# Attention outputs of a delta-rule kernel computed already transposed, in two column tiles, with their last rows moved by DMA

## The chip, the core and the metric

The kernel runs on one core of one Trainium2 chip. A core has TensorE (PE: matmuls; PEld: its weight loads), VectorE (DVE), ScalarE (ACT), GpSimd (POOL) and SyncE (SP), which only issues DMAs here. Each engine works through its own queue in order, and semaphores tie the queues together. TensorE writes to PSUM only; ScalarE and VectorE copy from PSUM to SBUF. The metric is the device time of one launch in microseconds.

## The reference

Two blocks run one after the other. The first is a delta rule over 4 batches x 8 heads, 768 steps, with heads 48 wide; the second is an MLP on its outputs.

```python
k_n = k / (norm(k) + 1e-6)
for t in range(768):
    y[t] = q[t] @ state                       # 48 x 48 state of each head
    v_old = state.T @ k_n[t]
    state += beta[t] * outer(k_n[t], v[t] - v_old)
x = y with heads side by side                 # 3072 tokens x 384
h = x @ w_in                                  # 384 x 2048
out = (h * sigmoid(1.702 * h)) @ w_out        # 2048 x 384
```

w_in and w_out arrive as 64-bit floats (numpy makes them so), and the kernel converts them to fp32 on the chip. q, k, v and beta are fp32.

## The kernel before, in words

**Units.** The sequence is cut into 6 chunks of 128 steps. A *unit* is one chunk of one batch with its 8 heads, so there are 24 units, in the order chunk by chunk, four batches in each. Within a chunk the recurrence is a triangular system. It is solved in four blocks of 32 rows with the inverses of the 32x32 diagonal blocks.

**Per unit.** `prepare` transposes K and Q of the unit (L285) and computes their products G (psG, L299). It sends G out to DRAM and back as NT (L311, L317), so that the blocks of two units lie one per partition. `invert` inverts them on VectorE, in 15 steps for halves of 16x16 (L363, L367) and then products of the halves (L346, L347); the last step YS (L397) goes to DRAM and comes back as XB (L401, L406). One call inverts two units; with the first chunk it is all four.

The class `Step` then walks through a unit. `keys` (L427) puts K times the state into psR. For each block `above` (L438) adds the blocks above to psR, `rest` (L446, VectorE) subtracts psR from V, and `solve` (L450) multiplies V by the inverse; `solved` (L457, ScalarE) copies the result to U. `queries` puts Q times the state into psY, `state` (L469, L477) updates S_bd, and `outputs` (L481) adds G times U to psY. psY has 128 tokens as rows and 8 heads x 48 as columns. ScalarE copies it to x (L486). `transposed` then transposes x in three pieces of 128 columns (L491), and VectorE copies them to xT (L493). xT holds 384 features in three pieces of 128 partitions, for the 256 tokens of a pair of units.

The state S_bd of two heads is block diagonal, 128 x 96, so that one matmul of `with_state` serves two heads. The heads of a pair lie at partitions 0 to 47 and 64 to 111; the partitions between are zero.

**The MLP.** `hidden` (ph, L506) multiplies w_in by xT, with w_in as weights and 256 tokens as data (128 for the first pair), and ScalarE applies the activation (L511). `written` (po, L521) multiplies by w_out. VectorE copies the result (L528), and a DMA writes it out (L529).

**Order.** The outer loop runs over *slots*, 26 of them. Slot n works on three units at once: the last two blocks and the outputs of unit n-1 (A), the second block of unit n (B_), and the start of unit n+1 (D_). It also prepares unit n+4. In even slots from 2 to 20 it also spreads an inversion over its groups. A slot has seven *groups*. After the attention work of a group the loop takes MLP work from a queue: `take(todo / (7 - group))` with `share` = 20.8 us of it in a slot, by costs written in the code (1.3 per two matmuls of po or three of ph). Outputs are group 5, transposes group 6. After every second slot `hidden` of the finished pair and then `written` are appended to the queue.

The order in the source is not yet the order on the engines: a scheduling layer reorders instructions of all engines by its own estimates, except those wrapped in `pinned`. The order is fixed when the program is built.

**Weights.** w_in comes in 12 parts of 128 rows x 512 columns and w_out in 16 parts of 128 x 384, fetched by DMA (L215) into space that is still free. Each is converted by five operations on VectorE and one on ScalarE (`from_double`, L164 to L173). This goes on during the first slots. Dummy matmuls `warm` (L135) keep TensorE's clock up where there is no other work.

Of the kernel before, what the change touches and what calls it, by code (L numbers as in the profile page):

```python
# [18 lines left out]
def kernel(  # L19
# [19 lines left out]
    nc = tc.nc  # L39
# [10 lines left out]
    BS = 32  # L50
    NB = C // BS
    HB = 2
    NTH = HB * C
    FQ = 4
    GB = 4
# [2 lines left out]
    NA = W0  # L58

    NW, NA0, NY, NB0 = 80, 3, 48, 6  # L60
    NS = C * C + C
    assert S % C == 0 and H == 8 and D <= DP and DM == H * D == KC * 128
    assert B == 4 and B * H * NB == 128 and FC == 4 * FQ

    cpool = ctx.enter_context(tc.tile_pool(name="const", bufs=1))
    io = ctx.enter_context(tc.tile_pool(name="io", bufs=3))
# [109 lines left out]
    parts_in = KC * DFF // N_IN  # L176
    n_parts = parts_in + FC

    stages, taken = {}, {}

    def stage(part):
# [15 lines left out]
    def fetch(part, dma):  # L197

        if part < parts_in:
            j, f0 = part % KC, part // KC * N_IN  # L200
            src = moe_w_in[j * 128 : (j + 1) * 128, f0 : f0 + N_IN]
        else:
            f = part - parts_in
            src = moe_w_out[f * 128 : (f + 1) * 128, :]
        if src.dtype == F32:
            dma(out=target(part), in_=src)
        else:
            if (s := stage(part)) is None:
                raw = wk.tile([128, DM, 2], I32, tag="xT", name="raw", bufs=3)
            else:  # L210
                taken[part] = s
                raw = w_out.rearrange("p f d -> p (f d)")[:, s[0] : s[1]].bitcast(I32)
                raw = raw.rearrange("p (n o) -> p n o", o=2)
            stages[part] = raw
            dma(  # L215
                out=raw.bitcast(src.dtype).rearrange("p n o -> p (n o)"), in_=src
            )

    def target(part):
        if part < parts_in:  # L220
# [193 lines left out]
    class Step:  # L414
# [40 lines left out]
        def solved(self, blk, psU):  # L455
            r = slice(blk * BS, (blk + 1) * BS)
            nc.scalar.copy(self.U[r], psU[r])  # L457

        def queries(self):
            self.psY = bank("psY")  # L460
            if self.c > 0:
                self.with_state(self.psY, 1)

        def state(self):
            if self.c == NC - 1:
# [11 lines left out]
                nc.vector.tensor_tensor(St, psS[pr, :, hh, :], St, op=ALU.add)  # L477

        def outputs(self):
            for h in range(H):  # L480
                nc.tensor.matmul(  # L481
                    self.psY[:, h, :], lhsT=self.G[:, h, 1, :], rhs=self.U[:, h, :],
                    start=(self.c == 0 and h == 0), stop=True, skip_group_check=True,
                )
            self.x = wk.tile([128, DM], F32, tag="o", name="x")
            nc.scalar.activation(self.x, self.psY.rearrange("p h d -> p (h d)"), ACT.Copy)  # L486

        def transposed(self):
            psX = bank("psXT2", (128, KC, 128))
            for j in range(KC):  # L490
                nc.tensor.transpose(psX[:, j, :], self.x[:, j * 128 : (j + 1) * 128], ident)  # L491
            i = self.b % HB
            nc.vector.tensor_copy(self.xT[:, :, i * C : (i + 1) * C], psX)  # L493


    def hidden(xT, gT, t, cost):
# [73 lines left out]
    def slot(n, share):  # L570

        nonlocal inverting
        A, B_, D_ = steps.pop(n - 1, None), steps.get(n), None
        P = prepare(n + B) if B <= n + B < len(units) else iter(())
        m = n - HB
        if m >= 0 and m % HB == 0 and m + B < len(units):  # L580
            inverting = invert(*units[m + B], HB)
        left = WB[n + 1] if n + 1 < len(WB) else 0
        todo = share
        for group in range(7):
            if group == 0:
                if A:
                    for h in range(H):
                        A.above(2, h)
                    A.rest(2)
                next(P, None)  # L590
            elif group == 1:
                psU = bank("psU") if A else None
                for h in range(H):
                    if A:
                        A.solve(2, h, psU)
                    if B_:
                        B_.above(1, h)
                if A:
                    A.solved(2, psU)
                if B_:  # L600
                    B_.rest(1)
                next(P, None)
            elif group == 2:
                if A:
                    for h in range(H):
                        A.above(3, h)
                    A.rest(3)
                if n + 1 < len(units):
                    h = (n + 1) // HB
                    if h not in xTs:  # L610
                        xTs[h] = wk.tile([128, KC, NTH], F32, tag="xT", name="xT", bufs=3)
                    D_ = steps[n + 1] = Step(n + 1, xTs[h])
                    D_.keys()
                    D_.rest(0)
            elif group == 3:
                psU = bank("psU")
                turns = [(X, blk) for X, blk in ((A, 3), (B_, 1), (D_, 0)) if X]
                for h in range(H):
                    for X, blk in turns:
                        X.solve(blk, h, psU)  # L620
                for X, blk in turns:
                    X.solved(blk, psU)
                if A:
                    A.queries()
                next(P, None)
            elif group == 4:
                if A:
                    A.state()
                next(P, None)
                run(P)  # L630
            elif group == 5:
                if A:
                    A.outputs()
            elif A:
                A.transposed()
            ahead_of(inverting, 4)
            more = left // (7 - group)
            run(weights(more))
            left -= more
            if queue:  # L640
                for cost in take(todo / (7 - group)):
                    todo -= cost
            if not queue and n <= HB:
                warm(NB0)
        if n + 1 == len(WB) - 1:
            run(weights(n_parts))
        run(inverting)
        if n > 0:
            if n - 1 + B < len(units):
                load_values(n - 1 + B)  # L650
            m = n - 1 + len(KN)
            if m < len(units):
                load(m, ((KN, k), (QP, q)), sync if n < B else nc.sync.dma_start)
                normalize(m, nc.gpsimd.tensor_tensor)
            h = (n - 1) // HB
            if h == 0:
                i = (n - 1) % HB
                queue.append(hidden(xTs[h], gT0, slice(i * C, (i + 1) * C), 0.67))
            if n % HB == 0:
                gT = gT0 if h == 0 else []  # L660
                if h > 0:
                    queue.append(hidden(xTs[h], gT, slice(0, NTH), 1.3))
                queue.append(written(*units[h * HB], gT))
                xTs.pop(h)
# [29 lines left out]
        normalize(i, nc.gpsimd.tensor_tensor)  # L694
    run(weights(W1))
    for n in range(-1, len(units) + 1):
        slot(n, 20.8)
    run(take(1e9))


# [28 lines left out]
```

## Time and profile before

Median of 3 runs: 877.55 us (876.33 to 877.77). The profiled run took 876.47, its span is 874.6.

| what | from the page or an answer of the trace |
|---|---|
| busy share of PE, PEld, DVE, ACT, POOL | 95%, 72%, 56%, 23%, 12% |
| po L521, ph L506 | 267.5 us and 264.6 us of PE |
| outputs psY L481 | 384 records, 45.3 us; their weight loads 46.5 us |
| queries psY L427 | 160 records, 22.6 us |
| transposes psXT L491 | 72 records, 11.9 us |
| x copy L486 (ACT), xT copy L493 (DVE) | 24 x 489 ns, 24 x 552 ns |
| HBM to SBUF of a w_in part | 12 DMAs of 512 KB, 5.3 us to land |
| granted clock over the span | 0.973 (lower only at the start) |

How to read it. A matmul in fp32 appears as two records, so 24 units x 8 heads give 384 records in L481. The ends of PE records are modelled, so the distance from one start to the next tells more than the busy time. The number after a line's name counts records. A wait written in brackets at the end of a line names the engine and line that ended it.

### The profile page before, as it was taken

The numbers are of one execution on the slowest core, as the hardware profiler recorded it, in microseconds if no ns is written. First come the engines' busy times: TensorE is split into PE (matmuls) and PEld (weight loads), VectorE is DVE, ScalarE is ACT, GpSimd is POOL, SyncE is SP. The second block draws the span as 40 slices with busy tenths as digits, with TensorE's granted clock in tenths as the row PEclk, the third lists the DMA queues.
The fourth block names the chain that finished last, engine by engine and source line by source line (L and its number), as shares of the span: only waits on it lengthen the run. The fifth ranks groups of instructions, "written<-read, shape, count | busy, mean of one in ns | idle before, by whom it ended". The sixth has DMA issues, their size and how long they took to land.

```text
span 874.6 us, 15165 instructions
## 1 busy us (share of the span) xinstructions
PE 829.1 (95%) x6506; PEld 631.2 (72%) x6506; DVE 491.6 (56%) x1020; ACT 198.7 (23%) x363; POOL 102.2 (12%) x92
## 2 busy tenths in 40 slices
PE   8228999999999999999999999999999999999998
PEld 7116787668768768768768768768768778677684
DVE  7898889878871592591592591592591580110100
ACT  3103433332213213213213213113113112112020
POOL 2101111220030120120120120120100000000000
PEclk9659999999999999999999999999999999999999
DMA  9835643541222222222222232221121110000000
GB/s 239 211 60 116 163 134 85 128 103 31 53 70 40 49 58 52 49 66 44 49 61 49 48 70 41 48 64 40 38 61 31 31 40 13 10 10 1 10 10 18
DMA packets 159299, 54.56 MB, mean 62 GB/s; under 512 B 127232, under 2 KB 154880, under 8 KB 159232
## 3 DMA queue, kind: packets, MB, share of 16 engines
q1 hardware_dynamic: 153104, 52.38, 25.8%
q10 hardware_dynamic: 6128, 1.21, 1.0%
q8 instruction: 51, 0.84, 0.4%
q14 instruction: 16, 0.13, 0.1%
HBM read 33.13 MB, written 20.45 MB: 61 GB/s over the span
## 4 chain that ended last, share of the span: by engine, by line
PE 87%; DVE 11%; issue 1%; DMA 1%; POOL 0%; ACT 0%; SPq 0%; DVEq 0%; POOLq 0%
PE po L521 29%; PE ph L506 27%; PE psG L299 5%; PE psR L438 5%; PE psY L481 4%; PE psU L450 4%; PE psT L285 3%; PE psR L427 2%; PE psY L427 2%; PE ps_warm L135 2%; PE psS L469 2%; DVE P L101 1%; DVE YB L101 1%; PE psXT L491 1%; DVE tmp L172 1%; DVE P L346 1%
## 5 line engine op out<-in xcount | busy, mean ns | idle before, releaser
L521 PE MATMUL po<-w_out,gT 128*128 128x384 f32 x768 | 267.5, 494 | 0.0
L506 PE MATMUL ph<-xT,w_in 128*128 128x256 f32 (+1 forms) x1248 | 264.6, 366 | 0.2 <-DVE xT L493 0.2
L506 PEld LDWEIGHTS ph<-xT,w_in 128*128 128x128 f32 x1248 | 217.8, 191 | 30.4 <-issue 5.3
L521 PEld LDWEIGHTS po<-w_out,gT 128*128 128x128 f32 x768 | 139.7, 190 | 86.4 <-issue 6.1
L446 DVE TENSOR_TENSOR V<-V,psR 32x384 f32<-32x384 f32 x92 | 50.7, 551 | 135.8 <-PE psR L438 130.3
L511 ACT ACTIVATE gT<-ph 128x512 f32<-128x512 f32 (+1 forms) x104 | 58.6, 564 | 218.6 <-PE ph L506 218.5
L135 PE MATMUL ps_warm<-ident 128*128 128x256 bf16 x290 | 42.3, 306 | 36.3 <-DVE ps_warm L101 33.2
L323 POOL TENSOR_SCALAR_AFFINE_SELECT G<-G 128x1024 f32<-128x1024 f32 x24 | 27.0, 1126 | 385.2 <-DVE G L307 150.9
L457 ACT COPY U<-psU 32x384 f32<-32x384 f32 x96 | 45.1, 469 | 113.7 <-PE psU L450 61.6
L438 PEld LDWEIGHTS psR<-U,G 32*32 32x32 f32 (+2 forms) x1152 | 53.1, 108 | 19.0 <-issue 18.5
L135 PEld LDWEIGHTS <-ident 128*128 128x128 bf16 x290 | 31.0, 110 | 45.1 <-DVE ps_warm L101 34.3
L438 PE MATMUL psR<-U,G 32*32 32x48 f32 (+2 forms) x1152 | 62.7, 206 | 0.0
L299 PE MATMUL psG<-kqT 48*128 48x256 f32 x384 | 59.6, 402 | 2.9 <-ACT G L303 1.9
L450 PEld LDWEIGHTS psU<-V,XB 32*32 32x32 f32 x1536 | 37.5, 106 | 24.9 <-issue 9.1
L493 DVE COPY xT<-psXT 128x384 f32<-128x384 f32 x24 | 13.3, 552 | 70.6 <-PE psXT L491 70.4
L307 DVE COPY G<-psG 128x512 f32<-128x512 f32 x44 | 30.2, 689 | 40.3 <-PE psG L299 39.8
L363 DVE TENSOR_TENSOR P<-NT,YB 64x2 f32<-64x2 f32 (+4 forms) x150 | 49.1, 327 | 4.7
L367 DVE TENSOR_REDUCE YB<-P 64x2 f32<-64x2 f32 (+4 forms) x150 | 48.0, 320 | 4.7
L481 PEld LDWEIGHTS psY<-U,G 128*128 128x128 f32 x384 | 46.5, 192 | 4.4 <-ACT U L457 0.8
L450 PE MATMUL psU<-V,XB 32*32 32x48 f32 x1536 | 44.7, 204 | 2.3 <-DVE V L446 2.2
L299 PEld LDWEIGHTS psG<-kqT 48*128 48x128 f32 x384 | 36.2, 186 | 14.4 <-ACT G L303 3.1
L286 ACT ACTIVATE kqT<-psT 128x512 f32<-128x512 f32 x48 | 28.2, 600 | 76.7 <-PE psT L285 74.1
(78 smaller groups left out, 712.2 us busy)
## 6 DMA issues: line engine op xcount, KB each, us to landing
Nd<-G SPq DMA_DIRECT2D x24, 512.0 KB, 3.2
w_out<-in_moe_w_in_dram SPq DMA_DIRECT2D x12, 512.0 KB, 5.3
w_out<-in_moe_w_out_dram SPq DMA_DIRECT2D x14, 384.0 KB, 3.3
KN<-in_k_dram SPq DMA_DIRECT2D x24, 192.0 KB, 2.8
V<-in_v_dram SPq DMA_DIRECT2D x24, 192.0 KB, 3.2
out_dram<-o SPq DMA_DIRECT2D x24, 192.0 KB, 2.0
QP<-in_q_dram SPq DMA_DIRECT2D x21, 192.0 KB, 3.0
NT<-Nd SPq DMA_DIRECT2D x24, 128.0 KB, 2.5
```

What stands on the lines that cost most here:

```text
L135: nc.tensor.matmul(ps, lhsT=ones[:, 0:128], rhs=ones, start=True, stop=True)
L299: nc.tensor.matmul(ps[hh][:, i], lhsT=kqT[pr, g + i, 0, :], rhs=kqT[pr, g + i, :, :], start=True, stop=True,)
L363: tt(P, diag(Nf, i * BS, [[0, i], [1, i]]), diag(Yf, 0, [[BS, i], [1, i]]), op=ALU.mult,)
L367: red(diag(Yf, i, [[BS, i]]), P, axis=AX.X, op=ALU.add, negate=True)
L438: nc.tensor.matmul(self.psR[r, h, :], lhsT=self.G[a, h, 0, r], rhs=self.U[a, h, :], start=(self.c == 0 and h == 0), stop=True, skip_group_ ...
L446: nc.vector.tensor_tensor(self.V[r], self.V[r], self.psR[r], op=ALU.subtract)
L450: nc.tensor.matmul(psU[r, h, :], lhsT=self.XB[r, h, :], rhs=self.V[r, h, :], start=True, stop=True,)
L457: nc.scalar.copy(self.U[r], psU[r])
L481: nc.tensor.matmul(self.psY[:, h, :], lhsT=self.G[:, h, 1, :], rhs=self.U[:, h, :], start=(self.c == 0 and h == 0), stop=True, skip_group_ ...
L506: nc.tensor.matmul(ph[:, u], lhsT=w_in[:, j, f * 128 : (f + 1) * 128], rhs=xT[:, j, t], start=(j == 0), stop=(j == KC - 1),)
L511: nc.scalar.activation(gT[f0 // FQ][:, f0 % FQ : f0 % FQ + 2, t], ph, ACT.Gelu_apprx_sigmoid)
L521: nc.tensor.matmul(po, lhsT=gT[f // FQ][:, f % FQ, i * C : (i + 1) * C], rhs=w_out[:, f, :], start=(f == 0), stop=(f == FC - 1),)
```

## The change

psY is made transposed at once: 48 features of a head as rows and 128 tokens as columns. For this U, and in the queries the state, become the weights, and G or Q the data. Even heads write partitions 0 to 47, odd heads partitions 64 to 111, by turns: two column tiles of TensorE. So x, the transposes and their PSUM bank go, and a slot has six groups instead of seven.

psY has four pieces of 96 used rows, but xT has three of 128. The first three pieces go to xT by one copy per half (ScalarE the even heads, VectorE the odd ones). Heads 6 and 7, the fourth piece, are first copied to a tile `last` and then moved by six DMAs of 16 rows x 128 tokens to the free partitions 48 to 63 and 112 to 127 of the three pieces. The rows of w_in have to lie in the same order, so each of its parts comes in four DMAs (48, 16, 48 and 16 rows). In the first slots `share` is smaller, 15.6 and then 18.8, so that MLP work is kept for later slots.

```diff
+    GR = 6
+    XR = DP - D
+    def x_rows(j):
+        return [
+            (p + o, r, m)
+            for hh in range(2)
+            for p in (hh * 64,)
+            for o, r, m in (
+                (0, (2 * j + hh) * D, D),
+                (D, (2 * KC + hh) * D + j * XR, XR),
+            )
+        ]
...
-            dma(
-                out=raw.bitcast(src.dtype).rearrange("p n o -> p (n o)"), in_=src
-            )
+            raw = raw.bitcast(src.dtype).rearrange("p n o -> p (n o)")
+            for p, r, m in rows:
+                dma(out=raw[p : p + m], in_=src[r : r + m])
...
+        def turned(self, lhsT, rhs, start):
+            for h in range(H):
+                j, p = h // 2, h % 2 * 64
+                nc.tensor.matmul(
+                    self.psY[p : p + D, j, :], lhsT=lhsT(h), rhs=rhs(h),
+                    start=start and j == 0, stop=True, skip_group_check=True,
+                )
+
         def queries(self):
-            self.psY = bank("psY")
+            self.psY = bank("psY", (128, NP, 128))
             if self.c > 0:
-                self.with_state(self.psY, 1)
+                self.turned(
+                    lambda h: S_bd[h % 2 * 64 : h % 2 * 64 + D, self.b, h // 2, h % 2, :],
+                    lambda h: self.kqT[h % 2 * 64 : h % 2 * 64 + D, h // 2, 1, :],
+                    True,
+                )
...
         def outputs(self):
-            for h in range(H):
-                nc.tensor.matmul(
-                    self.psY[:, h, :], lhsT=self.G[:, h, 1, :], rhs=self.U[:, h, :],
-                    start=(self.c == 0 and h == 0), stop=True, skip_group_check=True,
-                )
-            self.x = wk.tile([128, DM], F32, tag="o", name="x")
-            nc.scalar.activation(self.x, self.psY.rearrange("p h d -> p (h d)"), ACT.Copy)
-
-        def transposed(self):
-            psX = bank("psXT2", (128, KC, 128))
-            for j in range(KC):
-                nc.tensor.transpose(psX[:, j, :], self.x[:, j * 128 : (j + 1) * 128], ident)
-            i = self.b % HB
-            nc.vector.tensor_copy(self.xT[:, :, i * C : (i + 1) * C], psX)
+            self.turned(lambda h: self.U[:, h, :], lambda h: self.G[:, h, 1, :], self.c == 0)
+            t = slice(self.b % HB * C, (self.b % HB + 1) * C)
+            last = wk.tile([128, 128], F32, tag="o", name="last")
+            for hh, copy in ((0, nc.scalar.copy), (1, nc.vector.tensor_copy)):
+                p = slice(hh * 64, hh * 64 + D)
+                copy(last[p], self.psY[p, KC, :])
+                copy(self.xT[p, :, t], self.psY[p, 0:KC, :])
+                for j in range(KC):
+                    nc.sync.dma_start(
+                        out=self.xT[hh * 64 + D : hh * 64 + DP, j, t],
+                        in_=last[hh * 64 + j * XR : hh * 64 + (j + 1) * XR],
+                    )
...
-        for group in range(7):
+        for group in range(GR):
...
-            elif group == 5:
-                if A:
-                    A.outputs()
             elif A:
-                A.transposed()
+                A.outputs()
             ahead_of(inverting, 4)
-            more = left // (7 - group)
+            more = left // (GR - group)
...
-        slot(n, 20.8)
+        slot(n, 15.6 if n <= B else 18.8 if n <= B + HB else 20.8)
```

## The prediction

> **What bounds the kernel now.** I read the page's busy times and chain first, then the chain in order of time, the busy times by stretch, and the timelines of TensorE and VectorE around one slot boundary.
>
> ```profile
> PE 829.1 (95%) x6506; PEld 631.2 (72%) x6506; DVE 491.6 (56%) x1020; ACT 198.7 (23%) x363; POOL 102.2 (12%) x92
> PE 87%; DVE 11%; issue 1%; DMA 1%; POOL 0%; ACT 0%; SPq 0%; DVEq 0%; POOLq 0%
> ```
>
> TensorE is the bound on the average. The chain in order of time shows the rhythm: two slots take 483.71 - 418.29 = 65.42 us.
>
> ```profile
> 418.29 1.72 PE psY L481 x16
> ...
> 450.98 1.72 PE psY L481 x16
> ...
> 483.71 1.72 PE psY L481 x16
> ```
>
> The stretches show that the slots of such a pair differ (columns: stretch, then busy us and instructions of PE, PEld, DVE, ACT, POOL, then clock):
>
> ```profile
> 398.00:431.00 33.00, 33.00 (x280) 27.00 (x281) 10.23 (x29) 8.93 (x16) 4.35 (x4) 1.00 0.18 39
> 431.00:464.00 33.00, 33.00 (x273) 23.28 (x269) 27.21 (x45) 6.00 (x11) 6.09 (x4) 1.00 0.31 67
> ```
>
> In the second, VectorE works 27.2 of 33 us: it inverts the blocks of a later chunk there. So the question is how much slack VectorE's queue has at the end of that slot. The TensorE timeline:
>
> ```profile
> 450.82 1.88 PE L481 MATMUL psY<-U,G 128*128 128x48 f32 x16
> 452.53 2.81 PE L521 MATMUL po<-w_out,gT 128*128 128x384 f32 x8
> 455.18 0.49 PE L491 MATMUL psXT<-ident,x 128*128 128x128 f32 x3
> 455.51 2.75 PE L521 MATMUL po<-w_out,gT 128*128 128x384 f32 x8
> 458.19 0.86 PE L438 MATMUL psR<-U,G 64*32 64x48 f32 x16
> 458.98 0.66 PE L285 MATMUL psT<-ident,KN 128*128 128x128 f32 x4
> 459.47 4.05 PE L506 MATMUL ph<-xT,w_in 128*128 128x256 f32 x18
> 463.45 0.23 PE L450 MATMUL psU<-V,XB 32*32 32x48 f32 x1
> ```
>
> and VectorE at the same moment:
>
> ```profile
> 456.81 1.22 DVE L397 TENSOR_TENSOR YS<-YB,bI 64x1024 f32<-64x1024 f32 x1
> 458.07 0.56 DVE L493 COPY xT<-psXT 128x384 f32<-128x384 f32 x1
> 459.56 0.17 DVE L243 TENSOR_SCALAR rn<-rn 128x8 f32<-128x8 f32 x1 [0.94 <-POOL rn L242]
> 460.44 0.55 DVE L446 TENSOR_TENSOR V<-V,psR 32x384 f32<-32x384 f32 x1
> ```
>
> The solve at 463.45 needs the V written at 460.44 to 460.99. It comes 2.4 us early. That slack is what the change spends.
>
> **What the Trainium skill says.** "TensorE: Matmul & The Clock Gate", section LDWEIGHTS: a weight load costs its columns over 1.2 GHz, not its rows. The trace agrees: psY L481 is 16 records in 1.72 us, 107 ns each for 128 columns, though its data (48 columns) are short. The same page, "Measured speedup vs the span model": three column tiles of 32 columns ran 2.38 times as fast. No run here shows tiles that share all 128 rows; row and column tiles that share nothing do overlap here (below). "TensorEngine Tiling (Array Packing)", Key Properties: a change of tiling mode drains the array. The trace fits: groups in other modes start the next group 0.1 to 0.2 us later than their matmuls account for.
>
> **The change, part by part.**
>
> *TensorE removed, per unit:* outputs L481 1.72 us (450.82 to 452.53), transposes L491 0.33 (455.18 to 455.51), queries L427 1.06 (441.30 to 442.36 in the timeline). Sum 3.11.
>
> *TensorE added, per unit.* An fp32 matmul takes two records: po with 384 columns takes 3.89/6 = 0.648 us, 1.69 ns a column. 128 columns: 0.213 us. Eight heads one after another: 1.71 us; two tiles side by side: 0.85, plus half a matmul of stagger (0.11) and 0.15 to 0.2 of mode change. That they go side by side: the 48 records of psU L450 in three tiles (48 columns, 80 ns alone for two records) take 0.81 us from 440.49 to 441.30, 34 ns a matmul; psU and psR in two tiles 25 ns a record, 50 a matmul. Queries use row and column tiles that share nothing, like these: I take 1.1 us. Outputs share their rows, which this trace doesn't show: 1.15 side by side, 1.86 in sequence; I take 1.15, by the skill's figure. Weight loads of 48 columns (0.08 us a matmul) lie below both. Saved: 3.11 - 2.25 = 0.86 us a unit (0.1 if the outputs go in sequence).
>
> *Copies and strips.* ScalarE and VectorE each get a 48x128 and a 48x384 copy in place of one 128x384: some 0.2 us more on each (estimate from 0.49 and 0.55 for 384 elements). Six DMAs per unit on SyncE's queue: 6 x 0.37 us of issue (its timeline) and 2 to 3 us to land (the DMA list: 2.0 for out, 3.2 for Nd). In the slot with the inversion, VectorE reaches `last` some 3.4 us after psY, the issues take 1.1 more, and landing 2.5: 7 us. In the built order the first ph that reads it stands behind two po groups of four matmuls, psR, psT, psU with psR, psT, the next psR and most of the keys, over 9 us: hidden. Queued behind these DMAs are V, KN and Yd loads, needed a slot later. At the end, eight po (5.2 us) cover copies (0.4 to `last`), six issues (2.2) and landing (2.0 to 2.5): 0 to 0.5 us lost.
>
> *w_in in four DMAs instead of one:* 36 more issues, 13 us of SyncE's queue, spread over the first 80 us; the first six parts took 8.0 us to issue for 6 DMAs before, against 24 x 0.37 = 8.9. Hidden by VectorE's conversions, which bound that stage.
>
> *One group fewer in a slot, and what waits.* This decides. In the built order of the new kernel, between the outputs and the solve that needs V stand four po, psR, psT, four po: 2.65 + 0.80 + 0.49 + 2.6 = 6.54 us. Before it was 463.45 - 452.53 = 10.9. VectorE's queue is not shorter. I count it from the end of psY that opens the inverting slot (t = 0). TensorE: six matmuls of ph, psR, psT, six ph and two po, then solve and psR end at 8.7. VectorE's order now has `V` (L465) after the 18-element product, so it sits idle from 6.3 until 8.85. From there the stretch that was 427.86 to 458.03 before, 30.2 us with 1.2 idle, runs without that V (-0.6) and with `last` and xT (+0.75): YS ends at 38.9. Then `rn` waits for GpSimd's pow, which starts after ssq at 37.65 and took 2.67 us (POOL timeline): 40.2. V ends at 40.9.
> TensorE: its other pieces of that slot, from the timeline, sum to 29.46; with 1.1 and 1.15 the outputs end at 31.7, and the solve wants V at 31.7 + 6.54 = 38.25. It waits 2.65 us. Everything behind it in TensorE's queue waits too. The rest of the pair, from the solve to the next psY, takes 22.9 + 2.25 = 25.15. A pair: 40.95 + 25.15 = 66.1 against 65.42, so **+0.7 us where 1.7 was saved**. The queue of an engine that was not the bound has become the bound.
>
> *Sum.* Five full pairs (units 7 to 16): +3.4. The pair after them has no ssq and rn, so V comes at 38.9, wait 0.75: -1.0. The last inverting pair, without psT and psG on TensorE: wait 2.4 against 1.7 saved: +0.7. Three last slots without inversion: -2.6; the last transposes -0.3. The beginning to the seventh outputs (287 us): until about 230 us it hangs on VectorE's conversions and two inversions, whose work there is the same within 1 us; four po slip from before the fifth outputs to after (+2.6), less 0.9 saved, and the next inverting slot ends like the later ones (+0.5): +2.3, uncertain by 5 either way, since conversions and V stand otherwise in VectorE's order. Total +2.5, less rounding: 877.55 + 2 = **879.5 us**.
>
> **The rivals.**
> *The saving comes through* (V on time): 0.86 x 20 units bound by TensorE = 17 us: 860. For it: TensorE shows no idle time in the stretches above. Against it: VectorE's 2.4 us of slack are less than the 4.4 us by which the path is cut.
> *The outputs don't overlap in their column tiles:* +0.75 in the slots where TensorE sets the pace, 11 of them: 888. For it: shared rows are not shown in the trace.
> *The strips are waited for:* if the DMAs queue behind others by 3 us more than counted, each pair loses some 2 to 3 us, 25 in all: 905. Against it: more than 2 us of margin.
>
> **How the numbers follow.** Main case 0.55, 872 to 887 around 879.5, by the beginning (5) and by 0.6 us a pair in VectorE's stretch: of it 0.09 faster by over 0.2%, 0.19 within, 0.27 slower. Saving comes through 0.28, all faster. No overlap 0.12, and strips 0.05, both slower. Together: faster 0.37, same 0.19, slower 0.44. The range has to reach into the first two rivals: 862 to 890; it leaves the strips out.
>
> **What would show it.** Right: in the new timeline TensorE has a gap of 2 to 3 us ahead of psU and psR once per pair, ended by VectorE's V; psY groups take about 1.1 us each; a pair takes 65.5 to 66.5; no ph waits for a DMA. Wrong: no gap at that solve and pairs of 63.7 (the first rival), output groups of 1.8 (the second), ph released by xT's DMA (the third), or a seventh psY moved by more than 6 us, which would put the cause in the beginning.

## The result, and the profile after

The changed kernel takes **904.43 us** (median of 4 runs, 902.04 to 905.79) against 876.94 (4 runs): ratio 1.031, 95% interval 1.0285 to 1.0336. The forecast was 879.5 with 862 to 890, so the measured time lies 25 us above it. From here on times inside a run are those of its profiled execution, whose span is 903.0 us (874.6 before). Two executions in the experiments, of 900.82 and 883.73 us, were over 1.5% slower than the fastest of their kernel; the medians count them, the ratios don't.

The page of the changed kernel, busy times and chain:

```profile
PE 829.3 (92%) x6564; PEld 614.9 (68%) x6564; DVE 499.7 (55%) x1044; ACT 201.9 (22%) x387; POOL 105.0 (12%) x92
...
PE 65%; DVE 24%; DMA 3%; issue 3%; POOL 3%; ACT 1%; SPq 1%; ACTq 0%; DVEq 0%
```

TensorE is busy as long as before (829.1), though its work has become less: part of the time its clock is halved, as shown below. Idle time grew from 45.5 to 73.7 us, and VectorE's part of the chain doubled from 11% to 24%. To find the places, I read the start of every unit's outputs (psY) from the timelines and subtract those of before:

| start of psY of unit | before | after | late by |
|---|---|---|---|
| 1 | 101.46 | 108.53 | 7.1 |
| 3 | 162.70 | 185.29 | 22.6 |
| 8 | 319.96 | 338.17 | 18.2 |
| 10 | 385.39 | 408.02 | 22.6 |
| 12 | 450.82 | 477.21 | 26.4 |
| 14 | 516.24 | 545.44 | 29.2 |
| 16 | 581.67 | 611.49 | 29.8 |
| 18 | 647.10 | 681.31 | 34.2 |
| 24 | 822.52 | 851.30 | 28.8 |

So there are two losses: 18.2 us in the beginning, and 16.0 us in the five pairs from unit 8 to 18. Then 5.4 us are won back.

**A pair.** TensorE of the changed kernel at the slot boundary that the prediction worked out (start, us, then what ended the idle time before in brackets):

```profile
408.02 1.08 PE L482 MATMUL psY<-G,U 128*48 128x128 f32 x16
409.04 2.85 PE L551 MATMUL po<-w_out,gT 128*128 128x384 f32 x8
411.81 0.86 PE L457 MATMUL psR<-U,G 64*32 64x48 f32 x16
412.61 0.66 PE L304 MATMUL psT<-ident,KN 128*128 128x128 f32 x4
413.10 2.75 PE L551 MATMUL po<-w_out,gT 128*128 128x384 f32 x8
418.35 0.28 PE L469 MATMUL psU<-V,XB 32*32 32x48 f32 x1 [2.51 <-DVE V L465]
...
419.77 1.11 PE L304 MATMUL psT<-ident,QP 128*128 128x128 f32 x4
420.68 0.58 PE L446 MATMUL psR<-S_bd,kqT 128*128 128x96 f32 x2
421.19 1.49 PE L457 MATMUL psR<-U,G 96*32 96x48 f32 x16
```

and VectorE at the same moment:

```profile
414.81 1.21 DVE L416 TENSOR_TENSOR YS<-YB,bI 64x1024 f32<-64x1024 f32 x1
417.54 0.17 DVE L262 TENSOR_SCALAR rn<-rn 128x8 f32<-128x8 f32 x1 [1.53 <-POOL rn L261]
417.75 0.55 DVE L465 TENSOR_TENSOR V<-V,psR 32x384 f32<-32x384 f32 x1
```

The gap is the forecast one. TensorE comes to the solve at 415.85, and V is written at 418.30, behind `rn` and its wait for GpSimd. What was not forecast is below the gap: psT takes 1.11 us instead of 0.66 and psR 1.49 instead of 0.86. TensorE runs at half its clock there. The stretches show it (columns as in the prediction; the clock is the third number from the right). The first lies around the slot boundary above, the second is the half-clock part of it, and the third lies around the only one of the five waits that was not followed by a slower clock:

```profile
398.00:431.00 33.00, 30.49 (x192) 22.18 (x187) 21.00 (x32) 6.04 (x12) 5.96 (x4) 0.90 0.31 69
...
418.50:425.10 6.60, 6.60 (x62) 5.92 (x61) 1.70 (x4) 1.07 (x2) 0.83 (x1) 0.50 0.53 101
...
531.00:564.00 33.00, 30.49 (x253) 21.17 (x252) 24.60 (x39) 6.09 (x12) 5.97 (x4) 1.00 0.31 68
```

The trace's clock record puts the half-clock stretches after the five waits at 350.1 (6.83 us), 418.4 (6.83), 490.1 (3.41), none, and 623.2 (6.83).

**The beginning.** SyncE's DMA issues before (start, length, what):

```profile
4.68 8.01 SPq L215 DMA_DIRECT2D w_out<-in_moe_w_in_dram  x6
14.90 0.38 SPq L101 DMA_DIRECT2D QP<-in_q_dram  x1
```

and after, where the same six parts are 24 DMAs:

```profile
4.72 18.04 SPq L236 DMA_DIRECT2D w_out<-in_moe_w_in_dram  x24
23.23 0.38 SPq L104 DMA_DIRECT2D QP<-in_q_dram  x1
```

The load of queries behind them is issued 8.3 us later, and TensorE waits 3.51 us for it, until 28.07:

```profile
28.07 0.66 PE L304 MATMUL psT<-ident,QP 128*128 128x128 f32 x4 [3.51 <-DMA QP<-in_q_dram]
```

The inversion of the first chunk (NT times bI on VectorE) begins at 35.79 before and at 42.20 after:

```profile
35.79 1.22 DVE L101 TENSOR_TENSOR NT<-NT,bI 128x1024 f32<-128x1024 f32 x1
...
42.20 1.22 DVE L104 TENSOR_TENSOR NT<-NT,bI 128x1024 f32<-128x1024 f32 x1
```

A second thing follows at 112 us:

```profile
111.59 0.60 PE L304 MATMUL psT<-ident,QP 128*128 128x128 f32 x4
112.99 0.70 PE L318 MATMUL psG<-kqT 48*128 48x256 f32 x2 [0.80 <-ACT kqT L305]
114.45 0.23 PE L469 MATMUL psU<-V,XB 32*32 32x48 f32 x1 [0.76 <-DVE V L465]
...
116.93 1.49 PE L457 MATMUL psR<-U,G 96*32 96x48 f32 x16
```

There are two short waits within 2.3 us, no filler between, and then 23.9 us of half clock, through unit 2's last solve and outputs and into the next slot. The clock is 0.50 in this stretch of the changed kernel

```profile
114.70:138.40 23.70, 22.91 (x225) 18.51 (x220) 12.55 (x32) 6.46 (x12) 2.09 (x2) 0.50 0.31 73
```

and 1.00 in the same stretch before:

```profile
114.70:138.40 23.70, 23.48 (x254) 20.91 (x253) 21.95 (x56) 9.79 (x21) 2.26 (x2) 1.00 0.51 126
```

(The kernel before runs at half clock too, but only from 28.5 to 66.0 us and three times for 3.41 us, the last up to 202.6.) Theory after this reading: two separate losses, each made larger by the clock, around a saving that is real. Rivals: the turned matmuls or the strips (the six DMAs for heads 6 and 7) make the pairs longer; the beginning comes from the strips' latency.

### The profile page after: what moved, and what is told of

It is laid out like the page before. It is cut to its first block, busy times and chain, and to the rows that moved or that the text cites. A ratio compares the mean times of both kernels' runs of the same rounds, so it can differ in the third digit from the quotient of the medians.

```text
span 903.0 us, 15752 instructions
## 1 busy us (share of the span) xinstructions
PE 829.3 (92%) x6564; PEld 614.9 (68%) x6564; DVE 499.7 (55%) x1044; ACT 201.9 (22%) x387; POOL 105.0 (12%) x92
## 4 chain that ended last, share of the span: by engine, by line
PE 65%; DVE 24%; DMA 3%; issue 3%; POOL 3%; ACT 1%; SPq 1%; ACTq 0%; DVEq 0%
PE ph L536 24%; PE po L551 18%; PE psR L457 5%; DVE P L365 4%; PE psG L318 4%; PE psY L482 4%; PE psU L469 4%; PE psR L446 3%; POOL rn L261 2%; DVE NT L366 2%; DVE YB L366 2%; DVE YB L386 2%; PE psT L304 2%; DVE P L382 2%; PE psS L501 1%
## 5 line engine op out<-in xcount | busy, mean ns | idle before, releaser
L536 PE MATMUL ph<-xT,w_in 128*128 128x256 f32 (+1 forms) x1248 | 271.9, 375 | 0.0
L536 PEld LDWEIGHTS ph<-xT,w_in 128*128 128x128 f32 x1248 | 224.9, 196 | 35.1 <-issue 7.5
L457 PEld LDWEIGHTS psR<-U,G 32*32 32x32 f32 (+2 forms) x1152 | 58.4, 115 | 20.3 <-issue 19.1
L138 PE MATMUL ps_warm<-ident 128*128 128x256 bf16 x260 | 36.5, 298 | 37.0 <-DVE ps_warm L104 33.1
L318 PE MATMUL psG<-kqT 48*128 48x256 f32 x384 | 66.4, 434 | 4.0 <-ACT kqT L305 2.2
L457 PE MATMUL psR<-U,G 32*32 32x48 f32 (+2 forms) x1152 | 68.9, 215 | 0.0
L138 PEld LDWEIGHTS <-ident 128*128 128x128 bf16 x260 | 26.8, 106 | 45.4 <-DVE ps_warm L104 34.3
L318 PEld LDWEIGHTS psG<-kqT 48*128 48x128 f32 x384 | 39.4, 201 | 16.3 <-issue 4.7
L558 DVE COPY o<-po 128x384 f32<-128x384 f32 x24 | 13.3, 553 | 62.7 <-PE po L551 62.5
L322 ACT ACTIVATE G<-psG 128x512 f32<-128x512 f32 x48 | 28.6, 596 | 67.0 <-PE psG L318 65.6
L261 POOL TENSOR_TENSOR rn<-ssq,half 128x8 f32<-128x8 f32 x18 | 35.5, 1970 | 49.1 <-DVE ssq L259 49.1
```

The source lines that it names most:

```text
L138: nc.tensor.matmul(ps, lhsT=ones[:, 0:128], rhs=ones, start=True, stop=True)
L261: nc.gpsimd.tensor_tensor(rn, ssq, half, op=ALU.pow)
L318: nc.tensor.matmul(ps[hh][:, i], lhsT=kqT[pr, g + i, 0, :], rhs=kqT[pr, g + i, :, :], start=True, stop=True,)
L457: nc.tensor.matmul(self.psR[r, h, :], lhsT=self.G[a, h, 0, r], rhs=self.U[a, h, :], start=(self.c == 0 and h == 0), stop=True, skip_group_ ...
L536: nc.tensor.matmul(ph[:, u], lhsT=w_in[:, j, f * 128 : (f + 1) * 128], rhs=xT[:, j, t], start=(j == 0), stop=(j == KC - 1),)
```

## Experiments on the pairs

**Seven groups again, from slot 7 on.** Outputs stay in group 5; group 6 has only MLP work and inversion steps.

```diff
+        GR = 7 if n > B + HB else 6
         for group in range(GR):
...
-            elif A:
-                A.outputs()
+            elif group == 5:
+                if A:
+                    A.outputs()
```

> The changed kernel, but from slot 7 on its slots have seven groups again: outputs stay in the sixth, the seventh holds only Mlp work, inversion steps. The slots up to 6 are untouched. Theory (the missing group): with the old distance from outputs to the solve that needs V, the wait of 2.5 to 3.1 us per pair goes, and with it the half-clock stretches that follow it (350, 418, 490 and 623 us in the changed kernel, 24 us in all, 12 us of work lost); five pairs then take about 63.7 instead of 66.5 to 69.6 us, and the time falls by about 22 us to 880 to 886. Rival (the transposed matmuls themselves, or the strips' DMAs, make the pairs longer): no change, 902 to 906. Middle: only the waits go, the clock still drops: 890 to 894.

Measured: 880.63 us (876.0 to 888.1 in 22 runs; ratio to before 1.0046, 1.0028 to 1.0064), 23.8 us below the changed kernel. TensorE now has four more matmuls of po and three of ph ahead of the solve:

```profile
400.31 1.08 PE L481 MATMUL psY<-G,U 128*48 128x128 f32 x16
401.32 5.43 PE L550 MATMUL po<-w_out,gT 128*128 128x384 f32 x16
406.68 0.86 PE L456 MATMUL psR<-U,G 64*32 64x48 f32 x16
407.48 0.66 PE L303 MATMUL psT<-ident,KN 128*128 128x128 f32 x4
407.97 2.75 PE L550 MATMUL po<-w_out,gT 128*128 128x384 f32 x8
410.55 1.46 PE L535 MATMUL ph<-xT,w_in 128*128 128x256 f32 x6
411.94 0.23 PE L468 MATMUL psU<-V,XB 32*32 32x48 f32 x1
```

VectorE writes V before that:

```profile
410.25 0.55 DVE L464 TENSOR_TENSOR V<-V,psR 32x384 f32<-32x384 f32 x1
```

TensorE reaches the solve 11.63 us after psY starts instead of 7.82. V comes at 10.5 or 11.2, no earlier than in the changed kernel (10.3 or 10.9). There is no idle time and no half clock between 300 and 650 us, and a pair takes 63.50 us. So the missing group was the cause in the pairs, and the saving of the turned outputs is there: 65.42 - 63.50 = 1.92 us a pair.

**Fillers in the gap.** V comes as late as before, but TensorE is kept busy.

```diff
+                    if n % HB == 1 and B + HB <= n <= len(units) - B:
+                        warm(22)
                     A.rest(2)
```

> The changed kernel with 22 bf16 filler matmuls (0.108 us each, 2.4 us, output not used) in each odd slot from 7 to 20, between the row sums of block 2 and the solve that waits for V, so that TensorE is busy where it stood idle. V comes no earlier. Theory (the idle gap makes the clock drop, and the drop costs on top of the wait): the half-clock stretches at 350, 418, 490 and 623 us vanish, the gaps shrink to under 0.7 us, the time falls by 10 to 13 us in the pairs and rises by up to 2.4 us for each odd slot without a wait (three late ones, up to 7): 893 to 901. Rival (the clock drops for another reason, or its drop costs nothing because the work behind it has slack): no fall, 904 to 912.

Measured: 895.25 us (893.44 to 901.69), 9 us below the changed kernel. The fillers stand where the gap was:

```profile
415.99 0.86 PE L457 MATMUL psR<-U,G 64*32 64x48 f32 x16
416.79 2.58 PE L138 MATMUL ps_warm<-ident 128*128 128x256 bf16 x22
419.20 0.60 PE L304 MATMUL psT<-ident,KN 128*128 128x128 f32 x4
```

There is no half clock from slot 7 on, and each pair takes 65.86 us instead of 68.63 on average. V is no earlier (10.3 or 10.9 us after psY). The fillers take 2.41 us, the waits took 2.85 on average, so 0.4 of the 2.8 us gained is idle time that a piece of ph, which is work done anyway, now fills. The other 2.3 us a pair are the clock's share, nearly half of the 5.1 that a pair lost against 63.50.

**Even heads first, then odd ones**, on top of the seven groups: column tiles not by turns.

```diff
-            for h in range(H):
+            for h in (0, 2, 4, 6, 1, 3, 5, 7):
```

> Seven groups from slot 7 on, but the heads of outputs and queries run as 0, 2, 4, 6, 1, 3, 5, 7, so that neighbours share a column tile instead of taking turns. Theory (turns make two matmuls run side by side): a group of 16 takes 1.8 to 1.9 us instead of 1.08, some 0.75 us more for each of the 44 groups, less what waits hide: 905 to 914. Rival (the overlap is not from the order): 879 to 882.

Measured: 902.07 us. The outputs take longer:

```profile
410.24 1.55 PE L481 MATMUL psY<-G,U 128*48 128x128 f32 x16
411.72 1.56 PE L550 MATMUL po<-w_out,gT 128*128 128x384 f32 x4
```

From one start to the next they take 1.48 us instead of 1.01, and the queries grow by the same 0.47. A pair takes 65.39 us, as before the change. So the turns are the whole saving in the pairs, though less than I expected of them (0.47 and not 0.75 a group): eight matmuls in this order cost 1.48 us, not 1.86. By turns a matmul takes 0.13 us, less than the 0.213 that the prediction has for one alone, so the matmuls themselves overlap and not only their weight loads. Seven times 0.213 is 1.49, so the one change of tile in the serial order may explain its low price; that is an estimate, and no run tests it.

## Experiments on the beginning

**w_in's parts whole again**, in the changed kernel.

```diff
-            rows = x_rows(j)
+            rows = [(0, j * 128, 128)]
```

> The changed kernel with each part of w_in loaded by one DMA instead of four. The rows are then not in the turned order, so the hidden layer multiplies the right numbers by rows in the wrong order: its output is not the reference's, its work is the same. Theory (SyncE's queue in the first 30 us): the third query load is issued at about 15 instead of 23.2 us, NT is multiplied at 35.8 instead of 42.2, the first outputs come at 101.5 instead of 108.5 us; the time falls by 6 to 8 us, to 896 to 898, and by up to 12 more if the half-clock stretch of 24 us at 114.6 us goes too. Rival (the 7 us are absorbed later, as VectorE's conversions were to hide them): under 2 us, 902 to 904.

Measured: 886.5 us, 17.9 below the changed kernel. The query load is issued at 13.56, the inversion begins at 35.63, and unit 8's psY is 2.0 us late instead of 18.2. The waits for V and their half clocks in the pairs are still there.

**Only the cuts, in the kernel before.**

```diff
+            cuts = [(0, 48), (48, 64), (64, 112), (112, 128)]
...
+            for p, e in cuts:
+                dma(out=raw[p:e], in_=src[p:e])
```

> The kernel before with nothing changed but the loads of w_in: each part in four DMAs of 48, 16, 48 and 16 rows, the rows in their old order. Theory (SyncE's queue): the third query load is issued 8 us later, the inversion of chunk 0 starts 6 to 7 us later, and the time rises by 5 to 8 us, to 882 to 885. Rival (hidden by VectorE's conversions, as was forecast): 876 to 878. If the half clock of the beginning follows from the late prologue alone, up to 12 us more than the first.

Measured: 892.63 us (ratio 1.0167, 1.0148 to 1.0187), 15 us above the kernel before, nearly twice the 8 us of the theory's upper end, though inside what it left for the clock. The loss stands complete at unit 6 (+17.1 us) and stays to the end. The same with only the first six parts cut:

```diff
-            cuts = [(0, 48), (48, 64), (64, 112), (112, 128)]
+            cuts = [(0, 48), (48, 64), (64, 112), (112, 128)] if part < 6 else [(0, 128)]
```

> The kernel before with only its first six w_in parts cut into four DMAs (rows in their old order), the other six whole. Theory (the first 24 DMAs hold up the query load, the rest are hidden): the same loss as with all twelve cut, 890 to 893. Rival (half of it comes from the later parts): 882 to 887.

Measured: 886.05 us, 8.5 above before; the rival is right that the later parts count too. In the profile unit 1 is 10.2 us late and units 5 to 24 are 10.3: what the first 24 DMAs do is done before the first outputs. With all twelve parts cut another 6.4 us came between units 1 and 6; how the later parts cost them was not tested. SyncE with six parts cut:

```profile
4.72 20.02 SPq L219 DMA_DIRECT2D w_out<-in_moe_w_in_dram  x24
25.44 0.38 SPq L101 DMA_DIRECT2D QP<-in_q_dram  x1
```

**Number of DMAs, or narrow blocks of partitions?** From 13.5 us on, while these loads ran (to 22 us in the changed kernel, to 19 before), their 4096-byte packets took 271 ns on average when cut and 164 when whole. Four DMAs of every fourth row keep the number and spread each over all partitions:

```diff
+            cuts = 4 if part < parts_in else 1
+            for i in range(cuts):
+                dma(out=raw[i::cuts], in_=src[i::cuts])
```

> The kernel before with each part of w_in in four DMAs again, but every fourth row in each, so that each DMA of 32 rows spreads over all partitions, instead of blocks of 48, 16, 48 and 16 neighbouring rows (892.6 us). Theory (narrow blocks of partitions: the 4096-byte packets of the blocks took 271 ns on average where those of whole parts took 164): the packets are fast again, the query load is issued by 15 us, 876 to 880. Rival (the number of DMAs, four times as many to issue and to keep in flight): 890 to 894.

Measured: 889.89 us. My theory fell. At least half of the packets are quick again (median 159 ns, as with whole parts; it was 288 in the changed kernel), though their mean of 214 ns lies between. Yet the 24 DMAs take as long to issue:

```profile
4.81 20.81 SPq L218 DMA_DIRECT2D w_out<-in_moe_w_in_dram  x24
25.74 0.51 SPq L101 DMA_DIRECT2D QP<-in_q_dram  x1
```

The data moved at 183 GB/s between 13.5 and 22 us, against 388 with whole parts (13.5 to 19). The packets' time is 0.61 of what the 16 DMA engines had in that stretch, against 0.89 in the changed kernel, so full engines don't explain this run. What both ways of cutting share is 24 smaller DMAs in place of 6. Each takes 0.75 to 0.87 us of the queue here on average, though SyncE issues one in 0.38 us at quieter times.

**Two issuing engines**, on top of the seven groups: every second DMA of the first six parts from ScalarE.

```diff
+        dmas = [dma] * len(rows)
+        if len(rows) > 1 and part < 6:
+            dmas = [dma, nc.scalar.dma_start] * 2
...
+            for (p, r, m), d in zip(rows, dmas):
+                d(out=raw[p : p + m], in_=src[r : r + m])
```

> Seven groups from slot 7 on, and of the first six w_in parts every second DMA is issued by ScalarE instead of SyncE (12 each). Theory (SyncE's 18 us of issuing ahead of the third query load cost 6 to 9 us with what follows): the query load is issued at 14 to 16 us, NT is multiplied at 36 to 38, the time falls by 6 to 9 us to 872 to 875. Rival (ScalarE's own copies of the first transposes then wait behind its DMAs, or the engines of the DMA rather than the queue are full): 878 to 884.

Measured: 888.53 us, 8 above the seven groups alone. Both queues together are hardly faster. SyncE's 12 take 17.5 us where its 24 took 18.8, and the query load is issued at 23.03 instead of 24.13, not at the 14 to 16 of the theory. The Trainium skill says it in its overview, "Trainium Kernel Development and Optimization", Key Constraints: DMAs issued from several engines run on the same DMA engines, and only the issuing time is saved. The trace fits, and here hardly even that is saved. As the rival said, ScalarE is held up by its 12 DMAs. It makes its first copy of transposes only at 23.75, and TensorE stands idle for 7.90 us:

```profile
16.02 0.49 PE L137 MATMUL ps_warm<-ident 128*128 128x256 bf16 x3
24.41 0.69 PE L306 MATMUL psT<-ident,KN 128*128 128x128 f32 x2 [7.90 <-ACT kqT L307]
```

**Fillers in slot 2**, on top of the seven groups: that slot takes no MLP work but six fillers per group.

```diff
-            if queue:
+            if queue and n > HB:
                 for cost in take(todo / (GR - group)):
...
-            if not queue and n <= HB:
+            if n <= HB:
                 warm(NB0)
```

> Seven groups from slot 7 on (880.6 us) and, in slot 2 alone, six filler matmuls per group in place of the first Mlp work, which comes one slot later. There the changed kernel's TensorE has gaps of 0.80 and 0.76 us within 2.3 us, ahead of 24 us at half clock. Theory (those gaps set off the half clock, which costs half of its length because the recurrence waits for TensorE there): the long stretch vanishes or shrinks under 7 us and the time falls by 8 to 12 us, to 869 to 873. Rival (the stretch costs nothing, or the Mlp work deferred by a slot is lost at the end): 879 to 884.

Measured: 878.2 us (871.44 to 882.42, 14 runs), only 2.4 below. In the profiled execution (872.8) the long half-clock stretch is gone, 3.4 us of it are left after 90 us, and unit 8 is 0.4 us early instead of 16.9 late. But the MLP work that was put off is paid at the end. Behind the last psY stand 56 records of po in place of 24 (seven groups alone first, then with the fillers):

```profile
825.03 8.01 PE L550 MATMUL po<-w_out,gT 128*128 128x384 f32 x24
...
807.76 18.33 PE L550 MATMUL po<-w_out,gT 128*128 128x384 f32 x56
```

So most of unit 8's gain of 17.3 us is work put off and not clock saved. Unit 3 suggests that the stretch cost less than half of its length. In both of these runs, and with whole parts (a run below), unit 3's outputs start 11.2 to 11.6 us after VectorE ends the second inversion, that of chunk 1's first two units, on which the start of unit 5 in the same slot waits. From the end of the first inversion to the end of the second, VectorE takes 104.0 us with seven groups alone, 99.1 with the fillers as well, and 90.9 with whole parts. So some 5 us go with the stretch, and 8 remain without it: unit 3 is still 19.3 us late. This run also changes TensorE's order, so the split is rough.

With the two queues as well:

> Both of the two edits above together on top of the seven groups. Theory (separate losses): 862 to 866, below the kernel before, with all of the work and the rows in their turned order. Rival (the early start also moves the gaps, so that only one of the two counts): 869 to 873.

Measured: 883.84 us. Neither reading's number came, since the two queues lose by themselves.

## Together, and a version below both kernels

**Both repairs at once:** seven groups from slot 7 and whole parts of w_in.

> Both of the last edits at once: seven groups from slot 7 on and each part of w_in by one DMA (rows in the old order, so the hidden layer meets the wrong rows and the output is not the reference's; the work is the same). Theory (two separate losses, of 24 us in the pairs and 18 us in the beginning, around a saving that is real): they add, 904 - 24 - 18 = 862, range 859 to 865, below the kernel before. Rival (they share a cause, such as the clock): 870 to 880.

Measured: 858.31 us (ratio 0.9791, 0.9768 to 0.9814), a little below the sum of the two edits. So this is what the turned outputs bring when nothing else is paid for them, in a kernel that leaves out the order of w_in's rows. Unit 24 comes 19.4 us earlier than before, 16.3 of them gained from unit 7 on, 0.96 a unit.

**The share of 20.8 in every slot**, on top of this:

```diff
-        slot(n, 15.6 if n <= B else 18.8 if n <= B + HB else 20.8)
+        slot(n, 20.8)
```

> The kernel with seven groups and whole w_in parts (output not the reference's for the reason given there), with a share of 20.8 in every slot as before. Theory (the smaller shares of the first slots cost 1 to 3 us of filler): 858 to 862. Rival (they only move work later, and the pairs take it up): the same as with the changed shares within 1 us.

Measured: 884.73 us. Both readings were wrong by over 20 us. The beginning is as quick (unit 8 4.9 us early, 4.0 with the smaller shares), but the waits for V are back, with half clocks after them:

```profile
PE psU L468 <- DVE V L464: 14.6, 8, 2.6
```

(The three numbers are the total in us, the times and the longest.) With the larger shares the built order is another one: the second piece of po and the piece of ph no longer stand between outputs and solve. TensorE reaches the solve 9.20 us after psY (11.63 without), while V comes at 11.0 or 11.7. Seven groups alone do not guard the solve; what counts is the work between outputs and solve against VectorE's queue.

**Fewer DMAs ahead of the query load**, with w_in cut as it has to be. First: three parts ahead, seven more ahead of the inversion.

```diff
-    ahead(4)
-    run(weights(1))
+    ahead(3)
+    convert(staged.pop(0))
...
-    run(weights(W0 - 1, sync))
+    convert(staged.pop(0))
+    convert(staged.pop(0))
...
+    ahead(7, sync)
     run(invert(0))
```

> Seven groups from slot 7 on and the four DMAs per part of w_in kept, but only three parts (12 DMAs) are issued ahead of the third query load, and the next seven (28 DMAs) after the loads of values and keys, ahead of the inversion of chunk 0. Theory (what costs is the queue ahead of the query load, not the number of DMAs): the query load is issued at 14 to 16 us, the inversion begins at 36 us, and the time is within 3 us of the kernel with whole parts, 861 to 866. Rival (the cuts cost wherever they are issued, or later on the same queue): 872 to 880.

Measured: 879.66 us, within a microsecond of the seven groups alone and in the rival's range. The query load is issued at 16.70 and the inversion begins at 35.34, as wanted. But the built order now puts the transposes and psG of two units ahead of the first solve, which starts at 87.41 instead of 77.68 in the changed kernel, and 48 us at half clock follow (91.6 to 139.4). This run moved too much to tell the readings apart. So in the next one three parts go ahead and only three behind the first writes of the inversion's input. Up to the first outputs TensorE's order is then that of the seven groups alone, apart from one group of transposes.

```diff
     convert(staged.pop(0))
+    ahead(3, sync)
...
-    ahead(7, sync)
+    ahead(0, sync)
```

The call with 0 fetches nothing.

> The same without the fillers in slot 2: seven groups from slot 7 on, and three parts of w_in ahead of the third query load. Theory: 6 to 8 us below the seven groups alone, 872 to 875. Rival: 879 to 882.

Measured: **873.29 us** (869.24 to 883.73 in 11 runs; ratio 0.9946, 0.9925 to 0.9967), 7.3 below the seven groups alone and half a percent below the kernel before, with all of the work and the rows in their turned order.

```profile
4.76 11.83 SPq L235 DMA_DIRECT2D w_out<-in_moe_w_in_dram  x12
17.15 0.38 SPq L103 DMA_DIRECT2D QP<-in_q_dram  x1
```

Here 12 DMAs take 0.99 us each. Unit 1 is 2.0 us late instead of 6.7. Half clock stays at 129 to 136 and 146 to 156 us, and unit 8 is still 10.1 us late. With the fillers in slot 2 too:

> The turned outputs with three edits: seven groups from slot 7 on, fillers in place of Mlp work in slot 2, and only three parts of w_in (12 DMAs) ahead of the third query load, three more behind the first writes of the inversion's input. All of the work, rows in turned order. Theory (the loss at the start is what stands ahead of the query load): the inversion of chunk 0 starts 6 to 7 us earlier, 868 to 873, below the kernel before. Rival (the blocks' slow packets hold up the following transfers instead, as when seven parts were sent behind it): 877 to 882.

Measured: 878.37 us. The number is the rival's, but the query load is issued as early as without the fillers (17.07) and unit 1 is only 2.5 us late. The same 56 records of po stand at the end, so here the fillers in slot 2 cost more than they save.

## Why the prediction was wrong, point by point

- *TensorE's savings, "0.86 us a unit":* right. Measured 1.02 for outputs and 1.01 for queries from start to start (1.15 and 1.1 forecast), and 0.96 a unit from the pairs of 63.50. That tiles sharing their rows overlap is shown by the serial order, and with it the rival of outputs in sequence falls.
- *"It waits 2.65 us" per inverting pair:* right. 2.51 or 3.08 us, 14.3 in the five waits behind units 8 to 16. Counted as in the prediction, V ends at 40.99 us (40.9 forecast) and the outputs at 31.73 (31.7); the path to the solve is 6.81 (6.54). As they are written the terms for the end of YS add up to 39.2, not 38.9; measured 38.7.
- *"A pair: 66.1", "+0.7 us":* right for the one pair without half clock (units 14 to 16: 66.05 us), **wrong for the other four** (69.9, 69.2, 68.2, 69.8). **The step that failed here** is that the gap was priced at its length alone; what it does to the clock was put at nothing. Three stretches of 6.83 us and one of 3.41 at half speed lose half of 23.9 us: 12.0. The sum closes: 5 x -1.92 saved, +14.3 waited, +12.0 clock is 16.7, measured 16.0, forecast 3.4. The fillers show the cause, and their 2.3 us a pair agree with 12.0 / 5. How long each stretch came out was partly chance (last section).
- *w_in: "24 x 0.37 = 8.9", "Hidden by VectorE's conversions":* **the step that failed most.** The 24 DMAs took 18.04 us, and behind them stood the pinned query load, which I named nowhere. The price of an issue came from a quiet queue, although the same sentence has 8.0 us for six, 1.33 each. The conversions hide nothing, since in VectorE's pinned order two of the three early ones come after the copies of G that wait for this load.
- *The beginning, "+2.3, uncertain by 5":* +18.2 at unit 8. From the seven groups with cut to those with whole parts (same edits otherwise) unit 8 gains 20.9 us: 8.7 up to unit 1, where the query load is late, and 12.4 between units 1 and 3. In that second part the cut version has the 23.9 us of half clock, and half of it would be 11.9 us; but the agreement is chance at least in part, since without the long stretch, with fillers in slot 2, most of the loss was still there. So w_in's cuts are shown to be the cause, the late query load the way for the first part, and the way for the second part stays open. That the cuts alone, without turned outputs, cost 15 us shows that the strips are not needed to explain it. Why the two short waits line up only behind the late load is not settled.
- *Copies and strips, "hidden":* right in the pairs, no ph waits for xT. Sizes were off without effect: 0.58 us per issue (0.37), 1.8 to land (2 to 3). At the end TensorE doesn't wait for the strips either (0 to 0.5 us forecast).
- *Rivals:* "the saving comes through" (860) needed both repairs: 858.3. The rival that ended near the measured time, strips waited for (905), is refuted: no ph waits for them, so its number is right by luck. The sign of something else stood in the prediction, a seventh psY moved by more than 6 us; it moved by 19.2.

## What to carry to other kernels

Cost a wait on TensorE at its length plus half of the slow-clock stretch that it sets off; in this kernel's pairs that almost doubled it, from 14.3 to 26.3 us. When a DMA is cut into pieces, ask what is queued behind it, and take the price of a piece from a stretch where the queue is full. And when an edit shortens the bounding engine's work, check at each point where it meets another engine whether that one is ready; work between the two can be worth more than the time saved.

## What the runs showed of the hardware

- **Gaps under 3.4 us can halve TensorE's clock.** "TensorE: Matmul & The Clock Gate", "HAM oscillation", gives idle gaps above some 3.4 us as the thing to avoid. Here single gaps of 2.5 to 3.1 us were followed by 3.4 to 6.8 us at half clock in four of five cases, and filling them kept the clock up. Gaps of 0.80 and 0.76 us within 2.3 us were followed by 23.9 us. So the measurement decides here: shorter gaps matter too.
- **How a gap falls counts as well as how long it is.** In each trace the changes of the clock from 80 us on lie on a grid of 3.41 us, whose place differs from trace to trace. In the changed kernel the waits that left 2.37, 2.51 and 2.62 us of idle time in one cell of this grid were followed by 6.83 us at half clock. The other two straddled a border: 1.63 + 1.45 us was followed by 3.41, and 1.67 + 0.84 (the gap at 553.3) by nothing. In all 17 traces half clock followed each of the 19 cells at full clock with over 2 us idle, 36 of the 72 with 1 to 2 us, and 7 of the 3,698 with less (all from 80 us on). What else decides in the middle range is open.
- A half-clock stretch can go on with hardly any idle time in it: TensorE was busy for 22.9 of the 23.7 us shown above.
- Two column tiles that share all 128 rows, in fp32, overlap: 16 records of 128 columns take 1.01 us by turns, 1.48 us one tile after the other.
- Cut into four, loads of 512 KB moved at 182 to 226 GB/s between 13.5 and 22 us instead of 388, in narrow blocks or with every fourth row, from one queue or two. What limits them is not shown.
